# Fused attention, FFN and routed experts on one core: statistics of the next batch moved in the order of work

## The chip, the core and the metric

The program runs on one core of a Trainium2 chip. It works with five engines, each with its own in-order queue of instructions: TensorE (PE, with PEld for its weight loads), VectorE (DVE), ScalarE (ACT), GpSimd (POOL) and SyncE (SP), which only issues DMAs here. The metric is the device time of one execution in microseconds; less is better.

## The reference

Three stages follow each other over 8 batches of 3072 rows (24,576 rows of 256 values):

```python
scores = (1.0 / S) * np.matmul(z, z.transpose(0, 2, 1))      # z: 8 x 3072 x 64
attn = np.maximum(scores, 0.0) ** 2
x = u * np.matmul(attn, v)                                   # u, v: 8 x 3072 x 256
h = x @ w_in                                                 # 256 x 2048, float64 words
x = (h * np.cos(h)) @ w_out                                  # 2048 x 256
logits = (x / |x|) @ (emb / |emb|).T / tau                   # 8 experts
e = argmax(logits); gate = softmax(logits)[e]
out = gate * (np.maximum(x @ w1[e], 0.0) @ w2[e])            # 256 x 1024, 1024 x 256
```

Every matrix product is taken in float16 pairs (a high part and the rest), three products for one. Before a tensor is split it is scaled by a power of two, for which its largest absolute value or its largest sum of squares must be known over the whole tensor. That is what the statistics of this text are for: z and v of each batch, w_in and w_out, and w1 and w2 of each expert.

## The kernel before

The rows are handled in 48 chunks of 512 (`NC`), six to a batch (`NCB`). While chunk n goes through attention, chunk n-2 goes through the FFN (w_in, cosine, w_out) and the router; both are interleaved on TensorE. When the last chunks have passed the FFN, the experts run over gathered rows in slots.

The order of work is written out by hand. `Timeline` (L19) takes pairs of a planned time and a function: `tl.at(t, fn)` runs one function, `tl.at2(t, lead, load, fn)` runs its load `lead` earlier. All are sorted by time, and called in that order, which is the order of priority. On SP this order is kept as it is; the other engines' instructions are put in order by a scheduler from these priorities and from its own estimates, and each engine then executes its queue strictly in that order. `back` and `back2` (L166, L169) give a function the extra rule that its instructions come behind the newest piece of attention or FFN work on VectorE and ScalarE.

The names that matter here:

- `tB(n)` is the planned start of chunk n. For the preparation of batch b, `last` is the start of the last chunk of the batch before, and `P` its planned length, some 77,500 planned ns.
- `z_nat` (L434) loads z of a batch in three tiles, `z_stat` (L443) squares them on ScalarE, sums them on VectorE (`zns`) and takes the largest row (`znm`). `vpiece` (L469) loads one of twelve tiles of v, `v_stat_piece` (L493) squares it on ScalarE with an accumulated sum (`vstat`). `v_scale` (L507) sums these (`vm`). The tiles of these loads, of the conversions and of the weights come from one pool of five buffers (tag `st`); the loads go out on GpSimd's queue.
- `all_max` (L136) is GpSimd's all-reduce of a maximum over the 128 partitions. What follows it is `pow2_root` (L114) or `pow2` (L91): some seven VectorE operations on one column, each needing the one before. The first of them reads the all-reduce's result: `zpc<-znr`, `vsc<-vsr`. `w_scale` (L324) and `e_scale` (L405) do the same for weights and experts. In each of these functions the all-reduce and its first reader stand in one piece.
- In the router, `ro_hi` and `ro_lo` (L811, L823) write the float16 parts of a chunk's rows into the first 256 words of `row`; `ro_T` (L831) transposes these four times by DMA on SP into `xrT`; `ro_tail` (L837) copies the scale and the sum of squares (`amv`, `ssq`) into the last 16 words of the same tile; the logits (L855) multiply `xrT` on TensorE (`lg`) and write their differences into the tail too; `rank` (L902) counts rows by expert and scatters their numbers by four indirect DMAs on GpSimd (`idl_d`).
- The FFN's chain for one block of 512 x 128 is: three pairs of products on TensorE (`h`, L713), ScalarE's rounding (`kt`, L723), VectorE's fraction (L731), ScalarE's sine (L739), VectorE's product (`kt`, L743), ScalarE's and VectorE's halves (`gh` L748, `gl` L754), then twelve products on TensorE (`o`, L769). A block's `h` reuses a PSUM buffer that L743 of an earlier block must have read.

## Time and profile before

| | us |
|---|---|
| median of three runs | 5058.89 |
| lowest and highest of them | 5046.51, 5065.73 |
| the profiled execution | 5037.17 |
| its span, first to last instruction | 5035.4 |
| TensorE busy | 4872.0 (97%) |
| VectorE busy | 3553.7 (71%) |
| ScalarE busy | 3169.4 (63%) |
| GpSimd busy | 1509.1 (30%) |

The span has three parts: up to about 200 us the first batch is prepared and the weights are loaded, to about 3900 us attention and FFN run side by side, and behind that the experts alone. A row of instructions is told by its line in the kernel, its engine, its operation and what it writes and reads (`out<-in`). Behind it, in square brackets or behind the bar, stands the time that the engine sat idle just before it, and who ended that. The clock of TensorE is given as a share of 2.4 GHz, so 0.50 is its lower level of 1.2 GHz. A TensorE that is idle for a moment and one that runs at the lower clock are both lost time; idle time of another engine is lost only if TensorE waits for what comes behind it.

### The profile page before, as it was taken

Reading aid. Unit: us, or ns where it says so; the run is one execution under the profiler, and the core shown is the slowest. Engines: PE = TensorE matmul, PEld = TensorE weight load, DVE = VectorE, ACT = ScalarE, POOL = GpSimd, SP = SyncE. Lnnn points to the kernel's source line nnn. Section 1 sums busy time; section 2 is a strip of 40 time slices with the busy share of each in tenths; the row PEclk is TensorE's granted clock in tenths of the full one; section 3 lists DMA queues with packets and bytes.
Section 4 is the critical chain, followed back from the end, with each engine's and each line's share of the span. In section 5 each row is a group of like instructions: output and inputs, shape, how many; then the busy total and the mean of one; then the engine's idle time right before and its main releaser. Section 6 shows DMA issues by size and latency. Waiting matters only on the chain.

```text
span 5035.4 us, 86979 instructions
## 1 busy us (share of the span) xinstructions
PE 4872.0 (97%) x31032; PEld 2934.1 (58%) x31032; DVE 3553.7 (71%) x8946; ACT 3169.4 (63%) x5815; POOL 1509.1 (30%) x2105
## 2 busy tenths in 40 slices
PE   5999999999999999999999999999999799999999
PEld 2455555555555555555555555555556567777776
DVE  6877776777777768776877777687767556565555
ACT  6777776777777668776877777677767322222222
POOL 3232232232233224223322331332121433333332
PEclk9999999999999999999999999999999899999999
DMA  7677458546855685657556844774471767777874
GB/s 214 181 147 127 108 137 134 123 121 133 136 123 131 120 142 130 128 103 146 143 108 118 162 122 96 146 142 106 103 129 41 206 170 217 220 211 202 226 227 130
DMA packets 963687, 731.25 MB, mean 145 GB/s; under 512 B 855696, under 2 KB 858769, under 8 KB 954418
## 3 DMA queue, kind: packets, MB, share of 16 engines
q1 hardware_dynamic: 835490, 351.44, 35.8%
q0 software_dynamic: 127760, 374.24, 27.9%
q8 instruction: 243, 3.98, 0.4%
q14 instruction: 194, 1.59, 0.1%
HBM read 315.17 MB, written 215.19 MB: 105 GB/s over the span
## 4 chain that ended last, share of the span: by engine, by line
PE 66%; ACT 10%; DVE 9%; issue 7%; DMA 5%; POOL 2%; SPq 1%; POOLq 0%; DVEq 0%; ACTq 0%
PE acc L646 6%; PE acc L647 6%; PE acc L645 6%; PE h L713 4%; PE h L715 4%; PE h L714 4%; PE o L769 4%; PE o L777 4%; PE o L773 4%; PE h L1298 3%; PE o L1335 3%; PE o L1328 3%; PE o L1332 3%; PE h L1290 3%; PE h L1294 3%
## 5 line engine op out<-in xcount | busy, mean ns | idle before, releaser
L769 PE MATMUL o<-wo,gh 128*128 128x256 f16 x3072 | 839.3, 273 | 2.7 <-ACT gh L748 2.4
L773 PE MATMUL o<-wo,gh 128*128 128x256 f16 x3072 | 839.2, 273 | 0.0
L777 PE MATMUL o<-wo,gl 128*128 128x256 f16 x3072 | 838.8, 273 | 0.0
L739 ACT ACTIVATE kt<-kt,half_pi 128x512 f32<-128x512 f32 x768 | 550.9, 718 | 313.6 <-DVE kt L731 305.1
L748 ACT ACTIVATE gh<-kt 128x512 f16<-128x512 f32 x768 | 480.2, 626 | 422.0 <-DVE kt L743 409.6
L723 ACT ACTIVATE kt<-h,quarter,c 128x512 int32<-128x512 f32 x768 | 590.4, 769 | 205.8 <-PE h L715 165.4
L754 DVE TENSOR_TENSOR gl<-kt,gh 128x512 f16<-128x512 f32 x768 | 528.9, 689 | 258.7 <-ACT gh L748 246.1
L743 DVE TENSOR_TENSOR kt<-kt,h 128x512 f32<-128x512 f32 x768 | 524.7, 683 | 237.1 <-ACT kt L739 226.6
L731 DVE SCALAR_TENSOR_TENSOR kt<-h,c,kt 128x512 f32<-128x512 f32 x768 | 574.0, 747 | 161.6 <-ACT kt L723 145.8
L584 POOL DMA_DIRECT2D at_d<-ahl x480 | 267.3, 557 | 1258.9 <-DVE ahl L581 1055.3
L713 PE MATMUL h<-xh,wi 128*128 128x512 f16 x1536 | 585.6, 381 | 36.1 <-DVE kt L743 35.2
L1307 ACT ACTIVATE hh<-h 128x512 f16<-128x512 f32 x398 | 234.0, 594 | 563.5 <-PE h L1298 464.6
L714 PE MATMUL h<-xl,wi 128*128 128x512 f16 x1536 | 586.1, 382 | 0.0
L715 PE MATMUL h<-xh,wi 128*128 128x512 f16 x1536 | 585.5, 381 | 0.0
L646 PE MATMUL acc<-ahl,vh 128*128 128x512 f16 x1344 | 512.8, 382 | 24.0 <-DVE ahl L581 23.7
L645 PE MATMUL acc<-ahl,vh 128*128 128x512 f16 x1344 | 511.5, 381 | 16.7 <-ACT vh L367 6.0
L647 PE MATMUL acc<-ahl,vl 128*128 128x512 f16 x1344 | 512.3, 381 | 0.0
L1309 DVE SCALAR_TENSOR_TENSOR hl<-h,hh 128x512 f16<-128x512 f32 x398 | 271.6, 687 | 337.5 <-ACT hh L1307 292.6
L1328 PE MATMUL o<-w,hh 128*128 128x256 f16 x1592 | 435.9, 274 | 11.6 <-ACT hh L1307 7.4
L1335 PE MATMUL o<-w,hl 128*128 128x256 f16 x1592 | 436.0, 274 | 9.7 <-DVE hl L1309 5.2
L581 DVE TENSOR_TENSOR ahl<-r,ahl 128x512 f16<-128x512 f32 (+3 forms) x672 | 421.3, 631 | 33.8 <-ACT ahl L573 23.6
L1332 PE MATMUL o<-w,hh 128*128 128x256 f16 x1592 | 435.8, 274 | 4.1 <-issue 3.7
(327 smaller groups left out, 10138.1 us busy)
## 6 DMA issues: line engine op xcount, KB each, us to landing
w<-we_d SPq DMA_DIRECT2D x69, 2048.0 KB
at_d<-ahl POOLq DMA_DIRECT2D x480, 256.0 KB
vst<-in_v POOLq DMA_DIRECT2D x168, 256.0 KB
est<-in_w POOLq DMA_DIRECT2D x128, 256.0 KB
xs_d<-row POOLq DMA_DIRECT2D x48, 544.0 KB
ut<-in_uT POOLq DMA_DIRECT2D x42, 512.0 KB
zst<-in_zT POOLq DMA_DIRECT2D x84, 128.0 KB
ad_d<-ahl POOLq DMA_DIRECT2D x96, 96.0 KB
```

Of the source, the lines that this page charges most:

```text
L645: nc.tensor.matmul(out=acc[k], lhsT=h, rhs=ah, start=beg, stop=False)
L646: nc.tensor.matmul(out=acc[k], lhsT=h, rhs=al, start=False, stop=False)
L647: nc.tensor.matmul(out=acc[k], lhsT=lo, rhs=ah, start=False, stop=end)
L713: nc.tensor.matmul(out=ps, lhsT=wi_hi[:, k, fs], rhs=xh[:, k], start=(k == 0), stop=False)
L714: nc.tensor.matmul(out=ps, lhsT=wi_hi[:, k, fs], rhs=xl[:, k], start=False, stop=False)
L715: nc.tensor.matmul(out=ps, lhsT=wi_lo[:, k, fs], rhs=xh[:, k], start=False, stop=(k == KD - 1))
L723: nc.scalar.activation(out=kt, in_=h_t[n, f], func=ACTF.Identity, scale=xsc[n][0], bias=quarter)
L769: nc.tensor.matmul(out=o[t], lhsT=gh[:, ts], rhs=wo_hi[:, f], start=(f == 0 and t % 2 == 0), stop=False, skip_group_check=True,)
L773: nc.tensor.matmul(out=o[t], lhsT=gh[:, ts], rhs=wo_lo[:, f], start=False, stop=False, skip_group_check=True,)
L777: pe_last[0] = nc.tensor.matmul(out=o[t], lhsT=gl[:, ts], rhs=wo_hi[:, f], start=False, stop=(f == NF - 1), skip_group_check=True,).ins
L1328: nc.tensor.matmul(out=o[t], lhsT=hh[:, ts], rhs=wh, start=(f == 0 and t % 2 == 0), stop=False, skip_group_check=True,)
L1335: nc.tensor.matmul(out=o[t], lhsT=hl[:, ts], rhs=wh, start=False, stop=(f == NF2 - 1), skip_group_check=True,)
```

## The change

Three things are moved. The all-reduces (`z_max`, `v_max`, `w_max`, `e_max`) become functions with planned times of their own, ahead of the functions that read their results (`z_scale`, `v_scale`, `w_scale`, `e_scale`). `ro_tail` is planned ahead of the four transposes of a chunk's rows. The statistics of the next batch's z and v, which were planned 1.6 chunks before the boundary (z, in one piece) and in the half chunk before the last (v), are planned piece by piece over the three chunks before. The functions that are called do the same operations on the same data as before.

```diff
-    def e_scale(e):
+    def e_max(e):
         m = small.tile([128, 2], FP32, name="ewm", tag="ewm")
...
-        g = all_max(m, "ew")
+        ewst[e] = all_max(m, "ew")
+
+    def e_scale(e):
+        g = ewst[e]
...
-    def z_nat(b):
-        ts = []
-        for k in range(3):
-            t = st_p.tile([128, 512], FP32, name="znat", tag="st").rearrange("p (k d) -> p k d", d=DQ)
-            ks = slice(k * NJ // 3, (k + 1) * NJ // 3)
-            queue(b).dma_start(out=t, in_=z[b].rearrange("(p k) d -> p k d", p=128)[:, ks])
-            ts.append(t)
-        return ts
+    def z_nat(b, k):
+        t = st_p.tile([128, 512], FP32, name="znat", tag="st").rearrange("p (k d) -> p k d", d=DQ)
+        ks = slice(k * NJ // 3, (k + 1) * NJ // 3)
+        queue(b).dma_start(out=t, in_=z[b].rearrange("(p k) d -> p k d", p=128)[:, ks])
+        return t
...
+    def z_max(b):
         m = small.tile([128, 1], FP32, name="znm", tag="znm")
-        nc.vector.tensor_reduce(out=m, in_=ns, axis=AX.X, op=ALU.max)
-        zsc[b] = pow2_root(all_max(m, "zn"), "zp", 2.0 ** -20, 2.0 ** 8)
+        nc.vector.tensor_reduce(out=m, in_=zns.pop(b), axis=AX.X, op=ALU.max)
+        zsc[b] = all_max(m, "zn")
+
+    def z_scale(b):
+        zsc[b] = pow2_root(zsc[b], "zp", 2.0 ** -20, 2.0 ** 8)
...
+    def v_max(b):
+        m = small.tile([128, 1], FP32, name="vm", tag="vm")
+
+        nc.vector.tensor_reduce(out=m, in_=vstat[b], axis=AX.X, op=ALU.add)
+        vsc[b] = all_max(m, "vs")
+
     def v_scale(b):
-        m = small.tile([128, 1], FP32, name="vm", tag="vm")
-
-        nc.vector.tensor_reduce(out=m, in_=vstat[b], axis=AX.X, op=ALU.add)
-        vsc[b] = pow2_root(all_max(m, "vs"), "vs", 2.0 ** -50, 2.0 ** 13)
+        vsc[b] = pow2_root(vsc[b], "vs", 2.0 ** -50, 2.0 ** 13)
...
-            back2(last - ZS * P, LEAD, z_nat, z_stat, b)
+            for k in range(3):
+                back2(last - (3.3 - 0.25 * k) * P, LEAD, z_nat, z_stat, b, k)
+            back(last - 2.6 * P, z_max, b)
+            back(last - 2.4 * P, z_scale, b)
             for i in range(NJ // 2):
-                back2(last - 0.55 * P + i * 0.03 * P, LEAD, vpiece, v_stat_piece, b, i)
-            back(last - 0.05 * P, v_scale, b)
+                back2(last - (3.2 - 0.24 * i) * P, LEAD, vpiece, v_stat_piece, b, i)
+            back(last - 0.36 * P, v_max, b)
+            back(last - 0.2 * P, v_scale, b)
...
-    tl.at(t0 + 12500, w_scale, 0)
-    tl.at(t0 + 61000, w_scale, 1)
+    tl.at(t0 + 10700, w_max, 0)
+    tl.at(t0 + 13900, w_scale, 0)
+    tl.at(t0 + 58500, w_max, 1)
+    tl.at(t0 + 68000, w_scale, 1)
...
-        back(t0 + 8 * we / 22, e_scale, e)
+        back(t0 + 8 * we / 22, e_max, e)
+        back(t0 + 10 * we / 22, e_scale, e)
...
+        tl.at(r + 10300, ro_tail, n)
         for t in range(TT):
-            tl.at(r + 4300 + 2000 * t + late, ro_T, n, t)
-        tl.at(r + 11500 + late, ro_tail, n)
+            tl.at(max(r + 4300 + 2000 * t + late, r + 10310), ro_T, n, t)
```

VectorE at a batch boundary, before: the sum of the squares of v (`vm`), the reader of its all-reduce (`vsc<-vsr`) and the chain behind it, then the FFN's next operation (`kt`).

```order
L743 TENSOR_TENSOR kt<-kt,h 128x512
L754 TENSOR_TENSOR gl<-kt,gh 128x512
L510 TENSOR_REDUCE vm<-vstat 128x1
L514 TENSOR_SCALAR kq<-zpv 128x1
L118 TENSOR_SCALAR vsc<-vsr 128x1
L120 TENSOR_SCALAR vsh<-vsc 128x1
L125 TENSOR_SCALAR vsrt<-vsh 128x1
```

The same place with the change (line numbers are those of the changed kernel; `vm` is now at L520, the FFN's operations at L744, L756 and L767). Rows of the FFN and of attention, the router's and two conversions of z follow `vm`; the part up to the router's first rows stands here, and twelve more rows follow before `vsc<-vsr`.

```order
L520 TENSOR_REDUCE vm<-vstat 128x1
L744 SCALAR_TENSOR_TENSOR kt<-h,c_25049,kt 128x512
L756 TENSOR_TENSOR kt<-kt,h 128x512
L588 CAST ahl<-r 128x256
L594 TENSOR_TENSOR ahl<-r,ahl 128x256
L767 TENSOR_TENSOR gl<-kt,gh 128x512
L744 SCALAR_TENSOR_TENSOR kt<-h,c_25049,kt 128x512
L886 COPY lgs<-lg 128x64
L888 TENSOR_TENSOR dt<-lgs 128x32
```

The reader of the all-reduce stands 21 rows behind `vm` where it stood two rows behind it.

GpSimd at the same boundary, before: the store of the router's rows (`xs_d`), loads of v, the four scatters of row numbers (`idl_d`) and the all-reduce of v (`vsr`).

```order
L883 DMA xs_d<-row 128x4x272
L471 DMA vst<-in_v 128x2x256 x3
L132 DMA idl_d<-tok_i,psi 197120x1 x4
L138 ISA vsr<-vm 128x1
L471 DMA vst<-in_v 128x2x256
```

With the change:

```order
L603 DMA ad_d_77<-ahl 128x3x128 x2
L603 DMA ad_d_77<-ahl 128x2x128 x2
L138 ISA vsr<-vm 128x1
L603 DMA ad_d_77<-ahl 128x128 x2
L896 DMA xs_d<-row 128x4x272
L481 DMA vst<-in_v 128x2x256
L132 DMA idl_d<-tok_i,psi 197120x1 x4
```

The all-reduce has moved ahead of the scatters, and of the store of the rows, to a place between two stores of attention tiles (`ad_d`).

VectorE in the router of a chunk, before: the low halves of the rows (`row<-x`), then, some rows on, the two tail copies (`row<-amv`, `row<-ssq`).

```order
L826 SCALAR_TENSOR_TENSOR row<-x_26095,ams,row 128x256 x2
L743 TENSOR_TENSOR kt<-kt,h 128x512
L754 TENSOR_TENSOR gl<-kt,gh 128x512
L581 TENSOR_TENSOR ahl<-r,ahl 128x4x128
L731 SCALAR_TENSOR_TENSOR kt<-h,c_25020,kt 128x512
L841 COPY row<-amv 128x4x4
L842 COPY row<-ssq 128x4x4
```

With the change (the low halves are now at L839, the copies at L854 and L855):

```order
L839 SCALAR_TENSOR_TENSOR row<-x_26129,ams,row 128x256 x2
L854 COPY row<-amv 128x4x4
L756 TENSOR_TENSOR kt<-kt,h 128x512
L855 COPY row<-ssq 128x4x4
L767 TENSOR_TENSOR gl<-kt,gh 128x512
L594 TENSOR_TENSOR ahl<-r,ahl 128x4x128
L744 SCALAR_TENSOR_TENSOR kt<-h,c_25049,kt 128x512
```

The copies stand directly behind the low halves. The transposes keep their places on SP.

## Rows read from the trace of the kernel before

**Rows 1.** The page: its span line and the busy time of the engines.

```profile
span 5035.4 us, 86979 instructions
...
PE 4872.0 (97%) x31032; PEld 2934.1 (58%) x31032; DVE 3553.7 (71%) x8946; ACT 3169.4 (63%) x5815; POOL 1509.1 (30%) x2105
```

**Rows 2.** Two stretches: busy us (instructions) by engine, then clock, DMA share, GB/s.

```profile
600.00:800.00 200.00, 200.00 (x1205) 114.76 (x1204) 151.66 (x327) 146.40 (x257) 60.68 (x94) 1.00 0.63 129
200.00:3900.00 3700.00, 3646.67 (x22118) 2102.41 (x22117) 2750.72 (x5984) 2729.15 (x4970) 1043.02 (x1582) 1.00 0.61 125
```

**Rows 3.** Grouped instructions of VectorE: busy us, mean ns, idle before and its releasers.

```profile
L118 DVE TENSOR_SCALAR vsc<-vsr 128x1 f32<-128x1 f32 x8 | 1.2, 154 | 35.3 <-POOL vsr L138 24.5 <-issue 10.8
...
L841 DVE COPY row<-amv 128x16 f32<-128x16 f32 x48 | 8.6, 179 | 116.9 <-DMA xrT<-row 109.6 <-issue 7.2
```

**Rows 4.** VectorE in order of time at one boundary: start, us, instruction, idle before.

```profile
2304.12 0.15 DVE L118 TENSOR_SCALAR vsc<-vsr 128x1 f32<-128x1 f32 x1 [3.60 <-POOL vsr L138]
...
2305.51 0.74 DVE L731 SCALAR_TENSOR_TENSOR kt<-h,c,kt 128x512 f32<-128x512 f32 x1
```

**Rows 5.** GpSimd in order of time at the same boundary.

```profile
2302.77 0.96 POOL L132 DMA_INDIRECT idl_d<-tok_i,psi  x1 [0.30 <-issue]
2303.77 0.33 POOL L138 PARTITION_ALL_REDUCE vsr<-vm  x1
```

**Rows 6.** TensorE in order of time at the same boundary.

```profile
2307.78 0.58 PE L713 MATMUL h<-xh,wi 128*128 128x512 f16 x1 [3.12 <-DVE kt L743]
```

**Rows 7.** Four of seven stretches round the boundaries, and the sum of all seven.

```profile
862.00:877.00 15.00, 11.93 (x66) 6.90 (x65) 10.68 (x23) 8.11 (x12) 1.82 (x3) 0.89 1.08 88
1341.00:1356.00 15.00, 11.88 (x58) 6.45 (x57) 10.54 (x23) 8.19 (x12) 1.86 (x3) 0.77 1.21 71
1820.00:1835.00 15.00, 11.35 (x67) 6.34 (x66) 10.15 (x23) 8.10 (x12) 2.05 (x3) 1.00 1.28 103
...
3267.00:3287.00 20.00, 14.46 (x72) 7.90 (x71) 13.19 (x27) 8.72 (x13) 5.95 (x9) 0.83 1.22 93
sum 110.00, PE 83.78 PEld 47.50 DVE 76.27 ACT 57.45 POOL 19.57; mean PE 11.97 PEld 6.79 DVE 10.90 ACT 8.21 POOL 2.80
```

**Rows 8.** The sum of fourteen stretches round tail copies.

```profile
sum 237.00, PE 215.80 PEld 123.68 DVE 143.65 ACT 152.02 POOL 81.55; mean PE 15.41 PEld 8.83 DVE 10.26 ACT 10.86 POOL 5.82
```

**Rows 9.** Waits of TensorE: us in total, times, longest.

```profile
PE acc L645 <- DMA alm<-at_d: 2.9, 1, 2.9
```

**Rows 10.** VectorE at the tail copies of the last two chunks.

```profile
3928.24 0.17 DVE L841 COPY row<-amv 128x16 f32<-128x16 f32 x1 [17.23 <-DMA xrT<-row]
...
3968.29 0.17 DVE L841 COPY row<-amv 128x16 f32<-128x16 f32 x1 [9.80 <-DMA xrT<-row]
```

**Rows 11.** TensorE at the same places.

```profile
3926.84 0.19 PE L861 MATMUL lg<-en_r,xrT 128*128 128x16 f16 x1 [12.54 <-DMA xrT<-row]
...
3969.70 0.40 PE L1328 MATMUL o<-w,hh 128*128 128x256 f16 x1 [7.45 <-ACT hh L1307]
...
3974.15 0.17 PE L861 MATMUL lg<-en_r,xrT 128*128 128x16 f16 x1
```

**Rows 12.** Grouped instructions of ScalarE: the squares of v.

```profile
L501 ACT ACTIVATE vst<-vst 128x512 f32<-128x512 f32 x84 | 51.8, 619 | 2.9 <-DMA vst<-in_v 2.9
```

**Rows 13.** One stretch, in which the weights are loaded.

```profile
100.00:200.00 100.00, 87.18 (x403) 40.90 (x402) 78.33 (x164) 66.69 (x120) 33.93 (x54) 0.91 0.76 194
```

**Rows 14.** TensorE in order of time within it.

```profile
125.01 0.38 PE L646 MATMUL acc<-ahl,vh 128*128 128x512 f16 x1 [3.90 <-DVE ahl L581]
```

**Rows 15.** The all-reduce: duration ns min/median/max; who waited, us, times.

```profile
L138 POOL PARTITION_ALL_REDUCE xmr<-xm x48: 345/364/1003, 99.8 to 3834.4; - x48
...
L138 POOL PARTITION_ALL_REDUCE vsr<-vm x8: 308/324/380, 34.9 to 3270.3; - x8
...
  DVE e1c L95: 2.5, 5
```

**Rows 16.** DMA issues from 95 to 200 us: count, KB each.

```profile
w<-in_w_out POOLq DMA_DIRECT2D x13, 512.0 KB
```

More of the change, by code (lines that the diff above doesn't have):

```diff
@@ L322, in w_stat_piece, with w_max, w_scale @@
         )
-    def w_scale(which):
+    def w_max(which):
         m = small.tile([128, 1], FP32, name="wm", tag="wm")
         nc.vector.tensor_reduce(out=m, in_=wsc[which], axis=AX.X, op=ALU.max)
-        g = all_max(m, f"w{which}")
+        wsc[which] = all_max(m, f"w{which}")
+    def w_scale(which):
+        g = wsc[which]
         if wide:
@@ L432, in queue, with z_stat @@
         return nc.gpsimd if b else nc.sync
-    def z_nat(b):
-        ts = []
-        for k in range(3):
-            t = st_p.tile([128, 512], FP32, name="znat", tag="st").rearrange("p (k d) -> p k d", d=DQ)
-            ks = slice(k * NJ // 3, (k + 1) * NJ // 3)
-            queue(b).dma_start(out=t, in_=z[b].rearrange("(p k) d -> p k d", p=128)[:, ks])
-            ts.append(t)
-        return ts
-    def z_stat(ts, b):
-        ns = small.tile([128, NJ], FP32, name="zns", tag="zns")
-        for k, t in enumerate(ts):
-            nc.scalar.activation(out=t, in_=t, func=ACTF.Square)
-            nc.vector.tensor_reduce(
-                out=ns[:, k * NJ // 3:(k + 1) * NJ // 3], in_=t, axis=AX.X, op=ALU.add
-            )
+    zns = {}
+    def z_nat(b, k):
[3 more added lines that the diff above has]
+        return t
+    def z_stat(t, b, k):
+        if k == 0:
+            zns[b] = small.tile([128, NJ], FP32, name="zns", tag="zns")
+        nc.scalar.activation(out=t, in_=t, func=ACTF.Square)
+        nc.vector.tensor_reduce(
+            out=zns[b][:, k * NJ // 3:(k + 1) * NJ // 3], in_=t, axis=AX.X, op=ALU.add
+        )
+    def z_max(b):
         m = small.tile([128, 1], FP32, name="znm", tag="znm")
-        nc.vector.tensor_reduce(out=m, in_=ns, axis=AX.X, op=ALU.max)
-        zsc[b] = pow2_root(all_max(m, "zn"), "zp", 2.0 ** -20, 2.0 ** 8)
+        nc.vector.tensor_reduce(out=m, in_=zns.pop(b), axis=AX.X, op=ALU.max)
+        zsc[b] = all_max(m, "zn")
+    def z_scale(b):
+        zsc[b] = pow2_root(zsc[b], "zp", 2.0 ** -20, 2.0 ** 8)
     def zpiece(b, c):
@@ L831, in ro_T @@
     def ro_T(n, t):
-        row, sc, isc, ssq, xT = row_t[n]
+        row, xT = row_t[n][0], x2_t[n]
         nc.sync.dma_start_transpose(
@@ L954 @@
         if b == 0:
-            tl.at2(3700, 3700, z_nat, z_stat, 0)
+            for k in range(3):
+                tl.at2(3700 + k, 3700, z_nat, z_stat, 0, k)
+            tl.at(3710, z_max, 0)
+            tl.at(3720, z_scale, 0)
             for c in range(NCB):
@@ L971 @@
             pos = {j: i for i, j in enumerate(att_order(NCB - 1))}
-            back2(last - ZS * P, LEAD, z_nat, z_stat, b)
+            for k in range(3):
+                back2(last - (3.3 - 0.25 * k) * P, LEAD, z_nat, z_stat, b, k)
+            back(last - 2.6 * P, z_max, b)
+            back(last - 2.4 * P, z_scale, b)
             for i in range(NJ // 2):
-                back2(last - 0.55 * P + i * 0.03 * P, LEAD, vpiece, v_stat_piece, b, i)
-            back(last - 0.05 * P, v_scale, b)
+                back2(last - (3.2 - 0.24 * i) * P, LEAD, vpiece, v_stat_piece, b, i)
+            back(last - 0.36 * P, v_max, b)
+            back(last - 0.2 * P, v_scale, b)
             for c in range(NCB):
```

5 lines of the change are left out of this document (3 added, 2 removed).

## The prediction

> **What bounds the kernel now.** I read the page first [rows 1]: TensorE is busy 97% of the span, so only its idle time and its time at the lower clock can be won. Next come two stretches [rows 2]: a quiet one of 200 us has no TensorE idle at all, and from 200 to 3900 us it is idle 3700 - 3646.67 = 53.3 us. The kernel is a full TensorE queue with a few holes, and the question is which holes close.
>
> The grouped rows of VectorE name two suspects [rows 3]. The instruction that takes up the all-reduced maximum of v (`vsc<-vsr`) idles the engine 35.3 us over 8 instances, and the router's tail copy (`row<-amv`) idles it 116.9 us over 48. Whether that reaches TensorE is read from one such place in three engines. At a batch boundary VectorE stands still for 3.60 us until 2304.12, and its next FFN operation starts at 2305.51 [rows 4]. GpSimd was still sending four rank scatters when the maximum came up, and ran the 0.33 us all-reduce behind them [rows 5]. VectorE is in order, so `kt` is late and TensorE idles 3.12 us for it [rows 6]. Seven stretches round the seven boundaries hold 110 us, of which TensorE is busy 83.78: 26.2 us idle [rows 7]. Behind five of the stalls the granted clock drops to its 1.2 GHz level for a while, which shows in the means: 0.89 in three stretches of 15 us (that at 862 stands for them), 0.77 in another, 0.83 in one of 20 us. Lost: 3 x 0.11 x 15 + 0.23 x 15 + 0.17 x 20 = 11.8 us. Fourteen stretches round tail copies whose wait reached TensorE, those at the end of the FFN aside, hold 237 - 215.80 = 21.2 us of its idle time [rows 8]. Together that is 47.4 of the 53.3 us.
>
> **The change, part by part.** The count of instructions stays as it is on every engine; only places move. TensorE's sequence is the same but for some rows in the first few hundred microseconds, SP's is the same throughout.
>
> *Maxima of v apart from their use.* Between `vm` and the first reader of its all-reduce there now stand twenty VectorE instructions, and GpSimd reaches the all-reduce ahead of the scatters. The twenty hold two rounds of FFN products, by which more than the 3.6 us is covered, and the scatters are no longer in the 3.6 us. The nine small dependent operations that follow stay; they took 2305.51 - 2304.12 = 1.4 us. A halt of 3.6 + 1.4 = 5.0 us made TensorE idle 3.1, so some 1.9 us are slack and 1.4 us alone should not show. Gain: 26.2 + 11.8 = 38.0 us, less the 3.65 us of the stretch at 1820, which I keep, because a TensorE wait of that kind is for a stored attention tile and not for `kt` [rows 9]. That is 34.4 us. Ends: 38.0 if that stretch goes too, and 17 if boundary work is late next for half of it.
>
> *The tail copy ahead of the transposes.* The copy writes the last columns of the row tile, of which the transposes read the first ones. Written behind them it waited for their landing. Written ahead it needs only results of ScalarE and VectorE that are just being made, and the transposes, which SP issues some microseconds later, wait for two copies of 0.18 us. The `df` write behind the logits touches the same tile, but TensorE needs the landed transposes for the logits, so that wait is over by then. What the copy held up on VectorE is next in line without a wait. Gain: the 21.2 us; lower end 10, if half of these holes have another cause beside it, such as late ScalarE products.
>
> *The tail copies of the last two chunks.* The first waited 17.23 us, the second 9.80 [rows 10]. At the first, TensorE itself idles 12.54 us for the transposes [rows 11], which SP issues late, behind loads for the experts. Sequence and cause remain: 0. The second held up the gate's chain, then ScalarE's exp and relu, then TensorE for 7.45 us until 3969.70. Without it TensorE goes on at 3962.25. The 4.45 us of work that it did from there to the logits at 3974.15 take between half of that (had all of it run at the low clock) and all; it would be there at 3964.5 to 3966.7 and wait for transposes that landed just before 3968.29. Gain: 3974.15 - 3968.2 = 6.0 us; ends 0 and 7.5.
>
> *z and v statistics spread over three chunks.* The 84 squares of v take ScalarE 619 ns each and waited 2.9 us in all for a load [rows 12]. Spread out they stand beside FFN work, on a ScalarE that is busy 146.40 of 200 us [rows 2]: 0 in the steady part. For the second batch they fall into the loading of the weights. From 100 to 200 us TensorE is idle 12.8 us at a mean clock of 0.91 [rows 13], since VectorE waits in order for weight pieces, as before the stall of 3.90 us at 125.01 [rows 14]. Into that GpSimd queue now come z and v tiles of 128 x 512 x 4 bytes, 256 KB. At 194 GB/s, the rate of the stretch, one delays the next weight piece by 1.35 us. About two stand ahead of pieces whose lateness reaches TensorE, so I take +3 us. Ends: -4 (some weight reductions stand behind more useful operations than before, which could cover a stall of 3.90) and +11 (eight loads, all paid). The Trainium skill (DMA: Bandwidth & Descriptors, section Anatomy of one DMA — SWDGE (gpsimd) path) gives such a transfer a fixed 2 us plus its bytes over 436 GB/s, so an estimate by it is 0.6 us of queue a load and +1 instead of +3; the stretch's rate is less than half of that, and I go by the row.
>
> *All-reduces beside a busy VectorE.* Those of v ran while VectorE stood still (`vsr`: median 324 ns) and will run beside it. The rows have that case too: `xmr`, issued in the stream, has a median of 364 ns and a longest of 1003 [rows 15]. I take 0; the upper end is 24 moved all-reduces x 0.68 = 16.3 us of VectorE time, each under the slack of 1.9 us. The Trainium skill (SBUF — State Buffer, section Who interferes with whom) speaks against this edit: the two engines share a port pair as an exclusive lock, so that a GpSimd operation that reads SBUF and a VectorE one with two SBUF inputs block each other for a whole instruction. By it the sum would be worse by up to that end; the medians, 40 ns apart, do not show it.
>
> *Weight and expert maxima.* VectorE waited 2.5 us in all for those of the experts [rows 15], and not where TensorE did: 0.
>
> **Sum.** -34.4 - 21.2 - 6.0 + 3 = -58.6 us. The profiled execution took 5037.17 us (the span of 5035.4 and 1.8 around it), so 4978.6. The runs shown have a median of 5058.89, 21.7 above the profiled one. I forecast on their scale: 5058.89 - 58.6 = 5000.3, so 5000 us.
>
> **Rivals.**
> - *The boundary is late anyway.* ScalarE and VectorE are also loaded there with conversions of z and v, and attention tiles come late at 1820. Against it: `kt` is what TensorE waited for behind the maximum, and the waiting ended with it. If half of the boundary, tail-copy and last-chunk terms stay: -17 - 10 - 3 + 3 = -27, some 5032 us.
> - *The move does nothing.* GpSimd is in order and may stand before a v load whose buffer is not free when the maximum is ready, so that VectorE waits as before; and the transposes, now behind the copy, may be late for the logits. Against: at the boundary the new place is behind stores whose data VectorE makes before `vm`. The time would be 5045 to 5070.
> - *Slower: the weights starve.* Between 95 and 200 us 13 loads of w_out, 512 KB each, pass GpSimd's queue [rows 16]. If the new loads and reductions put each of them out of step, each costs TensorE a stall like that of 3.90 us, and more with the clock. The gains without the early term are 61.6 us; from 61.6 / 13 = 4.7 us a load the kernel is slower than before, and at 6 us it takes 5058.89 + 78 - 61.6 = 5075 us. Against: the whole stretch holds 12.8 us of idle now, with the same weight loads in it.
>
> **Chances and range.** Forecast 0.76, first rival 0.13, second 0.07, third 0.04. About 0.5% is what a measurement of this kernel can tell from no change, 25 us; faster means below 5033.6. The first rival's 5032 lies on that edge, and half of it counts there. Faster 0.82, same 0.14, slower 0.04. The lower end is 38.0 + 21.2 + 7.5 + 4 = 70.7 us off the profiled execution, the fastest time there is: 4966. The upper end takes in the first rival: 5034.
>
> **What would show it.** Right: in VectorE's rows no `vsc<-vsr` wait above 1 us and no `row<-amv` wait for `xrT`; TensorE idle below 15 us from 200 to 3900 us, with the clock at 1.00; the hole before `lg` near the end of the FFN still 12 us, and the one behind it about 4. Wrong: the boundary stretches keep their idle with another releaser (attention tiles, ScalarE's products), all-reduces of 0.7 us and more as a rule, or more than 20 us of idle from 100 to 200 us.

## The result

The changed kernel takes 4978.13 us (median of four runs, 4970.36 to 4986.71) against 5056.14 us for the kernel before on the same chip: a ratio of 0.9846, 95% interval 0.9819 to 0.9874, so 64 to 92 us less. The forecast was 5000 us, with a range of 4966 to 5034. The profiled executions lie closer together: the one of before lay under all its timed runs, and the one of after is the slowest of its own, 4986.71 us.

The page of the changed kernel, its span line and its engines [rows 1]:

```profile
span 4984.8 us, 87048 instructions
...
PE 4851.5 (97%) x31032; PEld 2931.0 (59%) x31032; DVE 3557.0 (71%) x8946; ACT 3170.9 (64%) x5815; POOL 1508.0 (30%) x2105
```

Three stretches of it (busy us and instructions by engine, then clock, DMA share, GB/s); the first two answer to [rows 13] and to the second of [rows 2]:

```profile
100.00:200.00 100.00, 70.84 (x317) 32.01 (x317) 66.39 (x145) 58.84 (x109) 34.74 (x54) 0.88 0.89 193
200.00:3900.00 3700.00, 3680.37 (x22445) 2130.86 (x22444) 2792.59 (x6075) 2762.59 (x5023) 1065.09 (x1606) 1.00 0.65 129
400.00:3800.00 3400.00, 3396.73 (x20658) 1960.62 (x20656) 2561.80 (x5527) 2552.71 (x4645) 982.71 (x1495) 1.00 0.64 127
```

In the middle, 400 to 3800 us, TensorE idles 3400 - 3396.73 = 3.3 us. From 200 to 3900 us it idles 19.6 us, most of it one hole near the end. From 100 to 200 us it idles 29.2 us, more than twice what it did.

VectorE's two suspects, in the grouped rows [rows 3] (busy us, mean ns | idle before them, releaser):

```profile
L854 DVE COPY row<-amv 128x16 f32<-128x16 f32 x48 | 8.5, 176 | 1.6
...
L118 DVE TENSOR_SCALAR vsc<-vsr 128x1 f32<-128x1 f32 x8 | 1.2, 148 | 7.7 <-POOL vsr L138 7.7
```

Both waits are gone: 116.9 us have become 1.6, and of 35.3 us the 7.7 are left that belong to the first batch, which waited as long before the change. The all-reduce itself [rows 15] takes little longer beside a busy VectorE than it took in the quiet (min/median/max ns):

```profile
L138 POOL PARTITION_ALL_REDUCE vsr<-vm x8: 347/357/378, 35.7 to 3202.0; - x8
```

The median rose by 33 ns, and TensorE is busy for all of the 15 us from 1 us ahead of each of the seven later readers. But the operation of VectorE beside each of the seven is `kt<-h,c,kt`, and its `h` lies in PSUM, the memory of TensorE's results, so that it reads one tile from SBUF. Of all 75 all-reduces of this kernel, the 19 that ran beside `ahl<-r,ahl` or `gl<-kt,gh`, which both read two SBUF tiles, have a median of 637 ns, the other 56 one of 357. One of the 19, GpSimd's row first, then VectorE's:

```profile
1033.36 0.64 POOL L138 PARTITION_ALL_REDUCE xmr<-xm  x1 [0.36 <-DVE xm L683]
...
1033.09 0.68 DVE L594 TENSOR_TENSOR ahl<-r,ahl 128x512 f16<-128x512 f32 x1
```

The all-reduce ends 0.23 us behind the VectorE operation, which is no longer than others (683 ns; the 528 of this shape have a median of 691). The Trainium skill (SBUF — State Buffer, section Who interferes with whom) describes an exclusive lock on a shared port pair, by which a GpSimd operation that reads SBUF waits while a VectorE operation with two SBUF inputs, issued first, runs; the trace agrees. The seven at the boundaries did not meet that case, and where it is met GpSimd pays some 0.3 us.

TensorE runs the same 31,032 matmuls in nearly the same order in all these kernels, so stages are compared best by when equal instructions start. The table gives the start of instruction 1600 (counted from 0), the time from there to 22,400 (attention with FFN), from there to 24,000 (last chunks, first experts), and from there to the last one, in us of each profiled execution:

| kernel | 1600 starts | to 22,400 | to 24,000 | to the last |
|---|---|---|---|---|
| before | 362.7 | 3490.5 | 257.3 | 915.8 |
| before again | 357.4 | 3510.0 | 261.0 | 890.4 |
| tail copy alone | 360.7 | 3461.6 | 252.6 | 890.4 |
| maxima of v alone | 357.1 | 3476.7 | 259.6 | 890.4 |
| spread alone | 369.7 | 3477.9 | 263.7 | 890.4 |
| spread and tail copy | 360.3 | 3427.9 | 254.2 | 890.4 |
| changed | 376.9 | 3423.6 | 255.4 | 920.4 |
| changed again | 367.6 | 3422.0 | 256.2 | 890.4 |
| second batch late (e4) | 365.9 | 3420.8 | 252.9 | 890.4 |
| weights' maxima back (e8) | 372.2 | 3420.5 | 252.2 | 890.4 |
| transposes before rows (e5) | 375.2 | 3421.3 | 256.2 | 890.4 |
| transposes before weights (e9) | 371.1 | 3420.2 | 262.3 | 890.4 |
| three edits (e10) | 364.1 | 3420.6 | 255.3 | 890.4 |
| both transposes early (e11) | 359.7 | 3420.7 | 254.3 | 912.1 |

Between the first profile of before and that of the changed kernel the stages give +14.1 (early), -67.0 (middle), -1.9 (end of the FFN) and +4.6 us (experts), -50 in all. The experts took 890.4 us in eleven executions and 912 to 920 in three, with the kernel before and the changed one in both groups: that is not of the change. The 50 us are less than the 78 between the medians because the first profile of before is a short execution of its kernel and that of the changed kernel the longest of its own.

### The profile page after: what moved, and what is told of

It reads as the page before. It is cut to its first block, busy times and chain, and to the rows that moved or that the text cites. A ratio compares the mean times of both kernels' runs of the same rounds, so it can differ in the third digit from the quotient of the medians.

```text
span 4984.8 us, 87048 instructions
## 1 busy us (share of the span) xinstructions
PE 4851.5 (97%) x31032; PEld 2931.0 (59%) x31032; DVE 3557.0 (71%) x8946; ACT 3170.9 (64%) x5815; POOL 1508.0 (30%) x2105
## 3 DMA queue, kind: packets, MB, share of 16 engines
q0 software_dynamic: 127760, 374.24, 29.2%
## 4 chain that ended last, share of the span: by engine, by line
PE 87%; DMA 4%; issue 3%; DVE 2%; ACT 2%; POOL 1%; another core or an unknown queue 0%; SPq 0%; POOLq 0%; ACTq 0%; DVEq 0%
PE acc L659 9%; PE acc L658 9%; PE acc L660 9%; PE o L782 6%; PE o L790 6%; PE o L786 6%; PE h L726 6%; PE h L728 6%; PE h L727 6%; PE h L1322 3%; PE o L1359 3%; PE h L1318 3%; PE h L1314 3%; PE o L1352 3%; PE o L1356 3%
## 5 line engine op out<-in xcount | busy, mean ns | idle before, releaser
L744 DVE SCALAR_TENSOR_TENSOR kt<-h,c,kt 128x512 f32<-128x512 f32 x768 | 574.5, 748 | 194.5 <-ACT kt L736 176.8
L756 DVE TENSOR_TENSOR kt<-kt,h 128x512 f32<-128x512 f32 x768 | 525.4, 684 | 253.2 <-ACT kt L752 240.7
L767 DVE TENSOR_TENSOR gl<-kt,gh 128x512 f16<-128x512 f32 x768 | 529.0, 689 | 237.0 <-ACT gh L761 222.9
```

## The experiments

**Which part does it?** Four kernels each hold some of the parts. The first is the kernel before with the tail copy moved:

```diff
+        tl.at(r + 10300, ro_tail, n)
         for t in range(TT):
-            tl.at(r + 4300 + 2000 * t + late, ro_T, n, t)
-        tl.at(r + 11500 + late, ro_tail, n)
+            tl.at(max(r + 4300 + 2000 * t + late, r + 10310), ro_T, n, t)
```

> The kernel before with the router's tail copy ahead of the transposes and nothing else of the change. Theory (each edit works by itself): the 116.9 us of VectorE waits at row<-amv go to under 5 us; TensorE loses the 21.2 us of holes at tail copies and about 6 us near the end of the FFN, so 5056 - 27 = 5029 us, and TensorE's idle time from 200 to 3900 us falls from 53 to some 32 us, what is left standing at the seven boundaries. Rival (those holes had late ScalarE products as a second cause): about half, 5043 us, with some 43 us idle. The early part up to 200 us stays as it was by both (12.8 us idle from 100 to 200 us).

Measured: 4976.35 us against 5016.61 on that chip, ratio 0.992 (0.9905 to 0.9935), 40 us less. The middle and a boundary stretch of it, as above:

```profile
400.00:3800.00 3400.00, 3375.08 (x20463) 1941.60 (x20462) 2537.92 (x5449) 2531.88 (x4605) 979.38 (x1490) 1.00 0.63 127
2284.00:2299.00 15.00, 11.90 (x73) 6.96 (x72) 8.41 (x21) 6.54 (x10) 4.80 (x6) 1.00 1.20 115
```

The copies' waits fell to 1.6 us and the boundary kept its 3.1 us of idle, as the theory has it; the size was wrong, 40 us for 27. The middle in the first profile of the kernel before, and in a second one (below):

```profile
400.00:3800.00 3400.00, 3353.16 (x20267) 1927.29 (x20266) 2514.04 (x5414) 2514.87 (x4584) 976.43 (x1485) 1.00 0.62 127
400.00:3800.00 3400.00, 3341.45 (x20151) 1917.53 (x20150) 2501.61 (x5393) 2503.63 (x4566) 971.09 (x1481) 0.99 0.64 126
```

TensorE idles 46.8 and 58.5 us there, and 24.9 with the tail copy moved; by the table the middle is 29 and 48 us shorter.

The second is the kernel before with the maximum of v alone taken apart:

```diff
-            back(last - 0.05 * P, v_scale, b)
+            back(last - 0.2 * P, v_max, b)
+            back(last - 0.05 * P, v_scale, b)
```

> The kernel before with the maximum of v taken 0.15 of a chunk ahead of its use and nothing else: the squares of v stay where they were, close to the boundary. Theory (the all-reduce behind the four scatters was the cause): the vsc<-vsr wait falls from 35.3 us to about the 8 us of the first batch, TensorE's idle time in the seven boundary stretches from 26 to under 5 us and the clock there to 1.00: 5056 - 35 = 5021 us. Rival (the boundary is overloaded by the squares and sums, and spreading them is what helps): the idle time there stays above 13 us with another releaser, and the time above 5038 us. Early part unchanged by both.

Measured: 5004.14 us, ratio 0.9975 (0.9964 to 0.9986), 12.5 us less. VectorE's wait and a boundary stretch:

```profile
L118 DVE TENSOR_SCALAR vsc<-vsr 128x1 f32<-128x1 f32 x8 | 1.2, 148 | 7.3 <-POOL vsr L138 7.3
```

```profile
400.00:3800.00 3400.00, 3358.58 (x20344) 1928.54 (x20343) 2521.21 (x5435) 2517.41 (x4588) 976.18 (x1488) 1.00 0.62 127
2283.00:2298.00 15.00, 14.14 (x84) 8.07 (x83) 10.97 (x29) 8.84 (x14) 6.28 (x7) 1.00 0.91 154
```

The wait went, and this boundary lost most of its hole (0.9 us of idle instead of 3.1). All seven together fell from 25.3 to 8.2 us, and the clock is 1.00 at each. But from 400 to 3800 us TensorE still idles 41.4 us: the holes outside the boundaries that end between the start of a tail copy's wait of over 1 us and 9 us behind it, 16.0 and 17.4 us in the two profiles of before, are 21.5 here, and stored attention tiles take their part. So the theory holds for the wait and the clock, and the time is that of the rival: what the boundary gave back was in part lost again further on.

The third is the changed kernel with the maximum again taken at its use:

```diff
-            back(last - 0.36 * P, v_max, b)
-            back(last - 0.2 * P, v_scale, b)
+            back(last - 0.05 * P, v_max, b)
+            back(last - 0.05 * P, v_scale, b)
```

> The changed kernel, but v's maximum is again taken directly ahead of its use at the old planned time (0.05 of a chunk ahead of the boundary); the squares stay spread. Theory (apart is what counts): the seven waits at vsc<-vsr come back, 3 us and more each, 25 us or more in all, and with them some 38 us of TensorE time: 4978 + 38 = 5016 us. Rival (spreading is what counts): no such loss, 4970 to 4985 us, since TensorE has slack when no squares stand at the boundary. Early part as in the changed kernel by both.

Measured: 4953.43 us, ratio 0.9873 (0.9856 to 0.9891). VectorE stands still as long as before at the boundary (start, us, instruction, idle before):

```profile
2262.45 0.15 DVE L118 TENSOR_SCALAR vsc<-vsr 128x1 f32<-128x1 f32 x1 [3.59 <-POOL vsr L138]
```

```profile
400.00:3800.00 3400.00, 3394.08 (x20656) 1957.84 (x20654) 2562.11 (x5523) 2552.99 (x4652) 980.65 (x1491) 1.00 0.62 127
2257.00:2272.00 15.00, 14.40 (x90) 8.59 (x88) 8.30 (x22) 6.77 (x10) 4.77 (x6) 1.00 0.78 73
```

The wait is back at all seven boundaries, and TensorE hardly notices: 0.6 us of idle in this stretch, 5.9 in the whole middle. The theory fell: the all-reduce behind the scatters released the wait, but the wait alone does not stop TensorE for long. (The profiled execution, 4943.29 us, is the shortest of this kernel's five.)

(In it the maxima of z, of the weights and of the experts stay apart from their use.) The fourth is the third with the tail copy back behind the transposes, so the spread alone:

```diff
-        tl.at(r + 10300, ro_tail, n)
         for t in range(TT):
-            tl.at(max(r + 4300 + 2000 * t + late, r + 10310), ro_T, n, t)
+            tl.at(r + 4300 + 2000 * t + late, ro_T, n, t)
+        tl.at(r + 11500 + late, ro_tail, n)
```

> The kernel before with the statistics of z and v spread over three chunks; v's maximum is read directly behind its all-reduce, and the tail copy stays behind the transposes (the maxima of the weights and experts are taken apart as in the changed kernel). Theory now (spreading gives the slack that the boundary lacked): the vsc<-vsr waits stay above 25 us, TensorE's idle time in the seven boundaries is under 5 us all the same, and from 363 to 3853 us it gains some 34 us. Rival (only both together, or the tail copy, free the boundary): less than 20 us, with 2 us and more of idle at most boundaries.

Measured: 5008.34 us against 5030.13 on its chip, ratio 0.9951 (0.9934 to 0.9968), 22 us less.

```profile
400.00:3800.00 3400.00, 3355.51 (x20342) 1930.05 (x20340) 2516.24 (x5435) 2514.45 (x4592) 977.71 (x1488) 1.00 0.65 127
2302.00:2317.00 15.00, 12.60 (x77) 7.30 (x75) 8.37 (x21) 6.63 (x10) 4.76 (x6) 1.00 0.73 76
```

This is the rival: six of the seven boundaries keep 2.4 us of idle or more, 17.7 us in all, and the middle is 12.6 us shorter than in the first profile of before (32 than in the second). Yet with the tail copy moved as well (the third kernel) the same stall is nearly free. What the spread changes is ScalarE ahead of the boundary. The stretch that begins 45 us before the reader of the maximum, in the kernel with the tail copy alone:

```profile
2244.00:2264.00 20.00, 20.00 (x119) 11.42 (x117) 13.23 (x26) 18.73 (x45) 6.38 (x10) 1.00 0.64 154
```

and in the kernel with spread and tail copy:

```profile
2217.00:2237.00 20.00, 20.00 (x119) 11.40 (x118) 13.90 (x31) 16.14 (x35) 2.56 (x4) 1.00 0.50 119
```

TensorE does the same 119 matmuls in both. In the first ScalarE is busy 18.73 of 20 us with the squares of v among the FFN's steps, in the second 16.14 (18.0 to 19.2 against 15.9 to 16.9 over the seven boundaries).

**The lead.** What both edits give TensorE can be read from the traces. The first product `h` of a block waits for VectorE's `kt<-kt,h` of the block two before: in the six profiles that have holes above 1 us ahead of an `h` ended by such an operation, it is that one in all 57. The time from the end of that operation to the start of the product is TensorE's lead. Just before the stall of [rows 4] it is 2299.30 - 2298.94 = 0.36 us (VectorE's row, then TensorE's):

```profile
2298.25 0.69 DVE L743 TENSOR_TENSOR kt<-kt,h 128x512 f32<-128x512 f32 x1
...
2299.30 0.38 PE L713 MATMUL h<-xh,wi 128*128 128x512 f16 x1
```

and at the same boundary of the third kernel 2261.76 - 2257.28 = 4.48 us:

```profile
2256.59 0.69 DVE L756 TENSOR_TENSOR kt<-kt,h 128x512 f32<-128x512 f32 x1
...
2261.76 0.38 PE L726 MATMUL h<-xh,wi 128*128 128x512 f16 x1
```

Means over the seven boundaries of the lead (of the blocks in the 40 us before VectorE stops, and of the last of them; where it does not stop, before the reader), and TensorE's idle time, summed over the seven stretches of 15 us that begin 1 us ahead of the reader, and from 400 to 3800 us:

| kernel | lead, 40 us | lead, last block | idle, boundaries | idle, middle |
|---|---|---|---|---|
| before | 1.0 | 0.4 | 25.3 | 46.8 |
| before again | 1.1 | 0.5 | 25.5 | 58.5 |
| tail copy alone | 2.3 | 1.2 | 21.7 | 24.9 |
| maxima of v alone | 1.1 | 0.5 | 8.2 | 41.4 |
| spread alone | 1.8 | 2.1 | 17.7 | 44.5 |
| spread and tail copy | 3.6 | 3.9 | 6.2 | 5.9 |
| changed | 3.3 | 3.8 | 0.0 | 3.3 |

In the kernels that keep the stall, last lead and idle time of one boundary add up to 4.0 to 4.8 us, near the 5.0 for which VectorE is held up. The stall costs what the lead does not cover, and each of the two edits brings a part of the lead. The tail copy's part is VectorE's own halts; that a full ScalarE is what takes the other part fits the rows above, but was not tested by itself.

The kernel before and the changed one were profiled once more:

> The kernel before once more, for a second profile of it on the chip of this series. Theory (what differs between executions lies in the loading of the weights and in the experts, not between them): up to 231 us and behind 3900 us it differs by several us from the first profile, and from 363 to 3853 us the times of equal TensorE instructions differ by less than 5 us. Rival (the waits of the middle part differ from run to run too): more than 10 us there.

Measured: 5029.65 us, at the median of its chip (5030.13), where the first profile lay under all timed runs. The middle took 3510.0 us, 19.5 more than in the first profile: the rival. With the same order of instructions TensorE idles 11.7 us more in it, and the mean clock is lower (0.99 for 1.00): before the change, how many stalls reach TensorE differs between executions, or between chips.

> The changed kernel once more, on the chip of this series. Theory (the first hundred VectorE rows of it are the same as in the run that read v's maximum at once, and that one lost nothing early): the 14 us lost before 231 us shrink to 0 to 5 us, TensorE is busy above 80 us from 100 to 200 us, and the time is 4 to 10 us below the 4953 us of that run, near 4945 us. Rival (the early loss belongs to the change): again 10 us or more lost there, 70 to 74 us busy, and a time above 4955 us.

Measured: 4949.92 us against 5030.13, ratio 0.9838 (0.9822 to 0.9854), the gain of the first chip. The middle is the same to 1.6 us, and the nine executions with the tail copy and the spread lie within 8 us of each other. The early loss was 4.9 us against the first profile of before (10.2 against the second, of the same chip), TensorE busy 78.36 us from 100 to 200 us: between theory and rival.

**The early part.** The changed kernel loses time while the weights load. GpSimd's queue there, with the first z and v tiles of the second batch among the weights:

```profile
128.22 0.54 POOL L445 DMA_DIRECT2D znat<-in_z  x1
...
131.74 0.71 POOL L312 DMA_DIRECT2D w<-in_w_out  x1 [2.44 <-DVE ahl L594]
...
133.01 0.71 POOL L481 DMA_DIRECT2D vst<-in_v  x1
...
146.46 0.53 POOL L312 DMA_DIRECT2D w<-in_w_in  x1 [12.18 <-ACT r L564]
```

VectorE and TensorE behind it:

```profile
143.69 0.69 DVE L452 TENSOR_REDUCE zns<-znat 128x8 f32<-128x512 f32 x1 [4.49 <-ACT znat L451]
...
152.68 0.69 DVE L319 TENSOR_REDUCE wst<-w 128x1 f32<-128x512 f32 x1 [6.77 <-DMA w<-in_w_out]
```

```profile
154.02 0.59 PE L659 MATMUL acc<-ahl,vh 128*128 128x512 f16 x1 [7.87 <-DVE ahl L594]
```

VectorE, in order, first waits 4.49 us for the square of the new z tile, then 6.77 us for the weight behind it, and TensorE 7.87 us for VectorE; the granted clock from 100 to 200 us is 0.88, for 0.91 before. Two kernels were to part the possible causes. The first (e4) is the changed kernel with the statistics of the second batch squeezed to 0.45 of their span, so that they start behind the weights (v's maximum and scale of that batch move to 0.22 and 0.1 of a chunk ahead of the boundary):

```diff
+            sq = 0.45 if b == 1 else 1.0
             for k in range(3):
-                back2(last - (3.3 - 0.25 * k) * P, LEAD, z_nat, z_stat, b, k)
+                back2(last - sq * (3.3 - 0.25 * k) * P, LEAD, z_nat, z_stat, b, k)
...
-                back2(last - (3.2 - 0.24 * i) * P, LEAD, vpiece, v_stat_piece, b, i)
+                back2(last - sq * (3.2 - 0.24 * i) * P, LEAD, vpiece, v_stat_piece, b, i)
```

> The changed kernel, but the statistics of the second batch alone are squeezed to start behind the loading of the weights (about 260 us instead of 120 us). Theory (the z and v loads and their in-order readers on VectorE hold up the last pieces of w_out): the 14.1 us that the changed kernel loses up to 231 us of the kernel before come back, 4978 - 14 = 4964 us, with TensorE busy about 87 us from 100 to 200 us as before (70.8 in the changed kernel). Rival (the early loss comes from the later scale of the weights, or is chance of one run): no change, 4975 to 4982 us, with TensorE busy below 77 us there.

Measured: 4937.85 us against 5016.61, ratio 0.984 (0.9824 to 0.9856), no better than the changed kernel's; instruction 1600 at 365.9 us, 79.2 us busy from 100 to 200 us. The second (e8) is the changed kernel with the weights' maxima back:

```diff
-    tl.at(t0 + 10700, w_max, 0)
-    tl.at(t0 + 13900, w_scale, 0)
-    tl.at(t0 + 58500, w_max, 1)
-    tl.at(t0 + 68000, w_scale, 1)
+    tl.at(t0 + 12500, w_max, 0)
+    tl.at(t0 + 12500, w_scale, 0)
+    tl.at(t0 + 61000, w_max, 1)
+    tl.at(t0 + 61000, w_scale, 1)
```

> The changed kernel, but the maxima and scales of w_in and w_out stand where the kernel before had them, each maximum directly ahead of its use. The statistics of the second batch stay early. Theory (the early loss is the z and v loads of the second batch among the weights): no change, again 5 to 14 us later than the first profile of the kernel before at equal TensorE instructions near 363 us. Rival (the new places of the weights' maxima cost it): that difference goes to -5 to +2 us, and the time falls by about 8 us.

Measured: 4942.59 us against 5015.1, ratio 0.9858 (0.9836 to 0.988); instruction 1600 at 372.2 us, 9.5 later than in the first profile. TensorE, VectorE and ScalarE run their instructions in the very order of the changed kernel, and GpSimd all of those of this stage: the edit moved nothing, so the new planned times of the weights' maxima can't be the cause, and this is the changed kernel once more. One execution does not decide here: with equal order of VectorE the stage ends anywhere from 360 to 377 us. Over the table the middle starts at 370.4 us on average in the seven executions with early statistics (360.3 to 376.9), and at 361.1 in the seven without (357.1 to 365.9): 9 us for z and v among the weights.

**The hole before the logits.** Its 11.29 us stand in the changed kernel as in [rows 11]:

```profile
3874.88 0.20 PE L874 MATMUL lg<-en_r,xrT 128*128 128x16 f16 x1 [11.29 <-DMA xrT<-row]
```

The rows were complete at 3845.5 us, and SyncE issued the transposes at 3868, behind those of the experts' rows:

```profile
3845.34 0.17 DVE L855 COPY row<-ssq 128x16 f32<-128x16 f32 x1
```

```profile
3858.11 5.16 SPq L1257 DMA_TRANSPOSE xT<-xg  x4
3865.33 0.33 SPq L1237 DMA_DIRECT2D w<-we_d  x1
3866.76 0.00 SPq L1239 DMA_DIRECT2D iw<-iw_d  x1
3867.59 0.34 SPq L1227 DMA_DIRECT2D ids<-idl_d  x1
3868.05 7.06 SPq L846 DMA_TRANSPOSE xrT<-row  x4
```

The next kernels move them forward. First ahead of the rows of the first group:

```diff
-        tl.at(max(t0 - 2.2 * Q, ready + 300), s_transpose, s)
+        tl.at(max(t0 - 2.2 * Q, ready + 300, T_X if s == 0 else 0.0), s_transpose, s)
```

(`T_X` is the planned time just behind the last of these transposes.)

> The changed kernel, with the four transposes of the first experts' rows on SyncE issued behind the router's transposes of the last chunk but one, instead of ahead of them. Theory (the transposes of the router waited on SyncE behind a wait for gathered rows, though their data had been there for 20 us): the hole of 11.3 us ahead of its logits closes, and the low clock behind it with it: 12 to 18 us less than the changed kernel beside it. Rival (the experts' rows, now later, stop TensorE next): the gain is given back at the first matmuls of the experts, less than 5 us.

Measured: 4947.75 us beside 4949.92 for the changed kernel: nothing. SyncE's queue and TensorE:

```profile
3845.94 0.33 SPq L1239 DMA_DIRECT2D w<-we_d  x1
...
3848.42 0.33 SPq L1239 DMA_DIRECT2D w<-we_d  x1
...
3850.62 14.90 SPq L846 DMA_TRANSPOSE xrT<-row  x4
```

```profile
3866.61 0.20 PE L874 MATMUL lg<-en_r,xrT 128*128 128x16 f16 x1 [9.57 <-DMA xrT<-row]
```

Issued 17 us earlier, the four transposes took 14.90 us to issue, behind two weight loads of 2 MB. By the Trainium skill (DMA: Bandwidth & Descriptors, section Queues, rings and completion order) SyncE has one ring on each DMA engine, consumed in ring order, so that the transposes stand behind those loads; the trace agrees, with 14.90 us behind them and 6.04 us ahead of them in the next kernel. Next, ahead of the weights as well (e9):

```diff
-        tl.at(max(t0 - 3.2 * Q, free, ready + 100), s_w, s)
+        tl.at(max(t0 - 3.2 * Q, free, ready + 100, T_X if s < 2 else 0.0), s_w, s)
```

> The changed kernel, with the router's transposes of the last chunk but one issued on SyncE ahead of the first two experts' weight loads and rows. In the last attempt they went ahead of the rows only, were issued at 3850.6 us and landed at 3866, behind 4 MB of weights issued just before. Theory (those 4 MB held them up): now they land by about 3853 us, the hole of 10 to 12 us ahead of the logits closes, and the clock stays at 1.00: 12 to 18 us less than the changed kernel. Rival (the weights or rows of the first expert come late instead): TensorE stops for them by about as much near 3880 us, less than 5 us gained.

Measured: 4947.63 us against 5015.1, ratio 0.9867 (0.9848 to 0.9886). The hole shrank to four gaps of 1.0 to 1.5 us, and the one before the last logits opened:

```profile
3836.99 3.71 SPq L1229 DMA_DIRECT2D ids<-idl_d  x4
3840.94 6.04 SPq L846 DMA_TRANSPOSE xrT<-row  x4
...
3906.48 0.33 SPq L1229 DMA_DIRECT2D ids<-idl_d  x1
3906.91 5.15 SPq L846 DMA_TRANSPOSE xrT<-row  x4
```

```profile
SPq L1229 <- DMA idl_d<-tok_i,psi: 19.9, 2, 16.1
```

```profile
PE lg L874 <- DMA xrT<-row: 26.6, 8, 18.4
```

The rows for the last chunk were complete at 3878.8 us. SyncE waited 16.1 us at a load of row numbers (the waits: us in total, times, longest), with the last transposes behind it, and TensorE 18.4 us. A kernel with this edit and the two on the early part (the diffs of e4, e8 and e9 together):

> Three edits on the changed kernel at once: the weights' maxima back (as in e8), the second batch's statistics behind the weights (as in e4), and the logits' transposes ahead of the experts' loads (as in e9). The first 300 VectorE instructions are then in the same order as in the kernel before. Theory: early part as before (-5 to +2 us against the first profile near 363 us), middle part as in the changed kernel (3421 to 3424 us between the same two TensorE instructions), the hole before the logits closed: 15 to 25 us below the changed kernel, ratio to the kernel before near 0.980. Rival (the early part is chance from run to run, and the transposes' gain is given back): ratio 0.983 to 0.985.

Measured: 4943.8 us, ratio 0.9858 (0.9838 to 0.9878): early part and middle as in the theory (+1.4 and 3420.6 us), and the transposes' gain given back, as in the rival, with the second hole at 13 us. Last, this kernel with that load and its gathers held until behind the last transposes:

```diff
+        held = s == 5
-        tl.at(max(t0 - 5 * Q, ready), s_ids, s)
+        tl.at(T_Y if held else max(t0 - 5 * Q, ready), s_ids, s)
...
-        tl.at(max(t0 - 4 * Q, ready + 200), s_gather, s)
+        tl.at(max(t0 - 4 * Q, ready + 200, T_Y + 1 if held else 0.0), s_gather, s)
```

(`T_Y` is for the last chunk what `T_X` is for the one before it.)

> The last kernel (three edits), and in it the load of row numbers for the sixth group of the experts, with its gathers, behind the router's transposes of the last chunk instead of ahead of them. In the last two runs the first hole before logits had closed, but SyncE then stood 16 us at that load, which waits for scatters, with the last chunk's transposes behind it, and TensorE idled 13 to 18 us for them. Theory (order on SyncE alone makes both holes): no hole above 3 us before either logits; the time from the 22,400th to the 24,000th TensorE instruction falls from 255 to 262 us in the changed kernel and the runs after it to about 240 us; 15 us below the changed kernel, a ratio of 0.980 to 0.983 to the kernel before. Rival (something third is late, such as the rows of the sixth group): the hole turns up at the experts' first matmuls, and the ratio stays at 0.984 to 0.986.

Measured: 4955.99 us against 5042.19, ratio 0.9834 (0.9814 to 0.9854). The 1600 instructions of this stage took 254.3 us, as ever. The holes shrank to 6.5 us and less, but gaps of up to 2.6 us came up, 7.1 us in all, that the trace puts down to no releaser:

```profile
3848.57 0.59 PE L727 MATMUL h<-xl,wi 128*128 128x512 f16 x1 [2.59 <-issue]
...
3851.37 0.59 PE L728 MATMUL h<-xh,wi 128*128 128x512 f16 x1 [2.21 <-issue]
```

Such gaps above 0.5 us stand behind instruction 22,400 in only three of the fourteen executions, the three with the long experts' stage (see the last section). So they need not come from this edit, and this run leaves open what it is worth. No version is shown to beat the changed kernel. In it and in the kernels made from it (e4, e5, e8 to e11) TensorE idles 23 to 33 us of this stage, at a mean clock of 0.93 to 0.95, whichever hole is closed; why the idle time moves and does not shrink is open.

## Why the prediction came out as it did

The time fell into the range, 4978 us measured for 5000 forecast, but the parts did not come as priced: two gave more than forecast and three less, and that their errors partly cancel is luck. So is the base. The parts were counted in a profile of before that lay 21.7 us under the median, and were taken off the median unchanged. Against that profile the change gave 50 us, in the second pair of profiles 83, between the medians 78 and 80, for 58.6 forecast.

- *Maxima of v, -34.4.* This step failed. It took the 26.2 us of idle and the 11.8 of clock at the boundaries as the price of one wait, with a slack of 1.9 us that stays as it is. The wait went, and the boundaries with it, but alone the edit brings 0.25% (12.5 us; 14 to 33 us of the middle against the two profiles of before), since part of the idle time came back behind the tail copies. And with the wait left in but tail copy and statistics moved, the seven boundaries idle 6.2 us: the slack is a lead of 0.4 to 3.9 us that other work decides. On top of the other two parts the edit is worth about 5 us of the middle by the profiles (3427.9 to 3422.8, the mean of the changed kernel's two), or 0.27 to 0.35% between the ratios of series on different chips.
- *Spread, 0 in the steady part.* This was the mis-sized term on the other side: 0.49% alone, although it costs some 9 us early. I had judged it by ScalarE's mean, 146.40 of 200 us in a quiet stretch [rows 2], and not by the stretch from 45 to 25 us ahead of a boundary, where it is busy 14.0 to 17.6 of 20 us in the kernel before and 18.0 to 19.2 once the tail copies are out of the way.
- *Tail copy, -21.2.* Mechanism right, size too small: 0.8% alone, 40 us, and 29 us of the middle even against the profile that it was counted in. I had counted only stretches in which the copy's own wait reached TensorE. The 2.4 us at each of 48 chunks, on average, also kept the lead small by which TensorE comes through other stalls, those of the boundary among them.
- *End of the FFN, -6.* The second wait vanished, as did TensorE's 7.45 us, and the hole before the first logits stayed, as said, with gaps of 3.6 us before the last ones for the 4 forecast. The stage gained 1.9 us here, 4.8 in the second pair: within the ends of 0 and 7.5.
- *Early part, +3.* 14.1 us in the profile of the forecast, 9 on average. The forecast priced queue time; what costs is VectorE waiting in order for a tile that is not there. So the Trainium skill's price for a load (DMA: Bandwidth & Descriptors, section Anatomy of one DMA — SWDGE (gpsimd) path), by which I had +1, and the row's rate both missed. The sign that I had named for this, over 20 us of idle from 100 to 200 us, did show.
- *All-reduces beside a busy VectorE, 0.* Right in size. But the reading that the medians do not show the lock was wrong: the 48 `xmr` mix both cases, some 640 ns beside a VectorE operation with two SBUF inputs and some 360 beside others.
- *Weight and expert maxima, 0.* Not measured alone; the new planned times of the weights' maxima moved nothing (e8).

The middle improved by 67 to 88 us for 55.6 forecast, which covered the early loss. TensorE's idle time from 200 to 3900 us, 19.6 us, missed the sign of 15. None of the rivals took place, but what the third described, weights that come late, did in small.

## What to carry to other kernels

When a full engine has several small holes behind different stalls, do not price each stall by the hole behind it: the engine comes to all of them with one lead, and the hole is what the lead does not cover. Measure the lead, from the end of what releases the engine to the start of its work, ahead of the hole; a stall that costs 3 us now may cost 1 us once others are gone, and one that costs nothing may be what keeps the lead small. (Measured alone, the three parts here do add up in the whole time: 0.80, 0.25 and 0.49% against 1.54 and 1.62% together. What failed is the price read from the holes.) Look for what is full in the tens of microseconds ahead of the hole, not on average over the stage. And a transfer that is moved forward on an in-order queue is early only if what stands ahead of it, in bytes and in waits, is early too.

## What was not expected of the chip

The experts' stage took 890.4 us to within 0.1 in eleven of fourteen executions and 912 to 920 in the others, with the same instructions. In the eleven TensorE does not idle in it at all; in the three it idles 15.7 to 21.9 us, most of it in gaps of about 1 us and less that the trace puts down to no releaser. The three are both profiles of the first series and the one of the last, in which the kernel before has its longest medians (5056 and 5042 us), so it may be of the chip as well as of the execution; the runs do not part the two. The kernel before had medians from 5015 to 5056 us on the chips of these series, while its ratio to the changed kernel was 0.9846 and 0.9838.
